# A delta-rule attention fused with a rational MoE: ScalarE's two reads of a unit's h side by side, four buffers for w, u and r, query products two slots later

## The chip, the cores and the metric

One core of a Trainium2 chip runs the whole program. PE is the matrix engine (TensorE), DVE the vector engine (VectorE), ACT the scalar engine (ScalarE), POOL is GpSimd, and SP is the engine that issues nearly all DMAs. Each engine takes its instructions strictly in the order in which they stand in its own queue, and waits for the others through semaphores. The metric is the device time of one execution in microseconds (us).

## The reference

A linear attention with a delta rule runs over 768 tokens for 4 x 8 heads of size 48; its output goes, token by token, through a two-layer network whose activation is a quotient of two polynomials of h.

```python
k_n = k / (norm(k) + 1e-6)
for t in range(S):                                  # S = 768, state is 48 x 48 for each head
    y[t]  = q[t] @ state
    v_old = state @ k_n[t]
    state = state + beta[t] * outer(k_n[t], v[t] - v_old)
x = y as [B * S, H * D]                             # 3072 x 384
h = x @ w_in                                        # 384 -> 2048
P = a0 + a1*h + a2*h**2 + a3*h**3
Q = 1 + |b0|*|h| + |b1|*h**2
out = (P / (Q + 1e-6)) @ w_out                      # 2048 -> 384
```

## The kernel before

The tokens are taken in 12 chunks of 64. A chunk of all heads passes through four pieces of attention code, each cut into 8 slots: `ahead` (loads and normalizes k), `front` (key products, the start of a triangular inverse, scales, transposed queries, query products), `middle` (off-diagonal blocks of the inverse, split of the state, residual, block-diagonal copies made by DMA) and `back` (solve in steps, next state, outputs, tokens, scalars). In one period of 8 slots `back` works on chunk c+1, `middle` on c+2, `front` on c+3 and `ahead` on c+4.

The network is cut into units: unit n is one chunk (256 columns) by 256 of the 2048 hidden features, so there are 8 units for each chunk and 96 in all. A unit is `hidden` (18 matmuls into one PSUM tile `ph`, of which there are two buffers), `numerator`, `quotient`, and `accumulate` (24 matmuls into `po`). The loop at the end writes numerator(n), quotient(n-1), one attention slot, accumulate(n-2) and hidden(n+1), in this order.

In `numerator`, L821 (ACT) reads `ph` and makes z in the buffer `mr`; L823 (DVE) reads z and `ph` and makes w in `mw`; L825 (ACT) reads `ph` and makes u in `mu`; L826 (ACT) takes the absolute value of w; L827 and L828 (DVE) read `ph` again and finish u. In `quotient`, L839 and L840 (ACT) make r by a logarithm and an exponential, in the buffer of z; L843 or L845 (DVE) makes the high half of g in `mg`, L846 (DVE) and L848 (POOL) or L850 (DVE) a remainder, and L851 (POOL) the low half of g. `mw`, `mu` and `mr` have `MB` buffers each; while the weights are loaded, the same three tags take the staged weights.

A scheduler sets the order of each engine's instructions before the program runs: it goes by the data's dependencies, by the buffers that are free, by priorities (code order, moved ahead where `high_priority` stands) and by times that it estimates. It also lets two engines that read the same PSUM tile do so one after the other, in code order. So an edit of a few lines can move instructions anywhere.

Three more tags matter. `g` (one buffer) holds the key products of L516, which two DMAs (L518) copy to DRAM, and later the masked query products `m32` of L655. `u0` (one buffer) holds `et` of L606's six DMAs. `sh` (two buffers) holds the state, split in two halves, which the residual's matmuls `pk` and the output's matmuls `py` read. `pk`, `pu`, `pd` and `py` take turns in one PSUM tile, and `pg`, `pm`, `pe` in another.

Of the kernel before, what the change touches and what calls it, by code (L numbers as in the profile page):

```python
# [10 lines left out]
F16 = mybir.dt.float16  # L11
F32 = mybir.dt.float32
BF16 = mybir.dt.bfloat16
U32 = mybir.dt.uint32
AF = mybir.ActivationFunctionType
# [21 lines left out]
def kernel(  # L37
# [12 lines left out]
    nc = tc.nc  # L50

    B, H, S, D = q.shape
    DM, DFF = moe_w_in.shape
    P = 128
    C = 64
# [7 lines left out]
    HP = NPAIR * H  # L63
# [1 line left out]
    NH = H // HG  # L65
    NG = NPAIR * NH
    TG = NPAIR * P
    MB = 3
    SHIFT = 2
    SHAPE = {  # L70
        "k": [P, NPAIR, 2, NH, 2, C, HG],
# [9 lines left out]
    sb = ctx.enter_context(tc.tile_pool(name="sb", bufs=2))  # L81
# [80 lines left out]
    a0, a1, a2, a3 = (coef[:, i : i + 1] for i in range(4))  # L162
# [60 lines left out]
    def split16(dst, src, scale=None, eng=None):  # L223

        if scale is None:
            nc.scalar.copy(dst[0], src)  # L226
        else:
            nc.scalar.activation(dst[0], src, AF.Copy, scale=scale)
        if scale is None:
            (eng or nc.vector).tensor_sub(dst[1], src, dst[0])  # L230
        else:
            nc.vector.scalar_tensor_tensor(  # L232
                out=dst[1], in0=src, scalar=scale, in1=dst[0], op0=ALU.mult, op1=ALU.subtract
            )
# [62 lines left out]

    STAGES = (("mw", MB), ("mu", MB), ("mr", MB))
    stage = [0]

    def staged(shape, dtype, nm):
        stage[0] += 1
        tag, bufs = STAGES[stage[0] % len(STAGES)]
        return sb.tile(shape, dtype, tag=tag, name=nm, bufs=bufs)
# [4 lines left out]
    def to_f32(t, src, nm, keep=MIN_NORMAL):  # L309

        n = t.shape[-1]
        st = staged([P, n, 2], U32, "ws" + nm)
        nc.sync.dma_start(out=st.rearrange("p f w -> p (f w)"), in_=src)
        wl, wh = st[..., 0], st[..., 1]
        a = sb.tile([P, n], F32, tag="mg", name="wa" + nm, bufs=MB)
        nc.scalar.activation(a, wh.bitcast(F32), AF.Abs)
        nc.gpsimd.tensor_scalar(a, a, 3.0e38, keep, op0=ALU.min, op1=ALU.max)
        nc.vector.tensor_scalar(
            t, a.bitcast(U32), 3, KEEP, op0=ALU.logical_shift_left, op1=ALU.bitwise_and
        )  # L320
        for word, scalar, in1, op0, op1 in (
            (wh, 0xC0000000, t, ALU.bitwise_and, ALU.bitwise_or),
            (wl, 29, t, ALU.logical_shift_right, ALU.bitwise_or),
        ):
            nc.vector.scalar_tensor_tensor(out=t, in0=word, scalar=scalar, in1=in1, op0=op0, op1=op1)  # L325
# [63 lines left out]
    def alternating(t):  # L389

        return t.rearrange("p g x a -> p g a x")

    def mm3(dst, bd, rt, start=True, stop=True):

        for p in PAIRS:
            mm3p(dst, bd, rt, p, start, stop)
# [13 lines left out]
    def bank(pool, nm, w):  # L410

        t = pool.tile([P, NPAIR, 512], F32, tag="a", name=nm)[:, :, : H * w].rearrange("x p (h w) -> x p h w", w=w)
        return t[:, 0], t[:, 1], t
# [5 lines left out]
    def parts_by_pair(t):  # L419
        return by_pair(t[:, 0]), by_pair(t[:, 1])  # L420

    def to_diagonal(nm, t, c=0):
        bd = diag[nm][c % len(diag[nm])]
        for b in range(2):
            sl = slice(b * C, (b + 1) * C)
            if nm == "kn":
                for a in range(HG):
                    nc.sync.dma_start(
                        out=bd[sl].rearrange("t p i (n a) b d -> t (p i n) a b d", a=HG)[:, :, a, b],
                        in_=t[:, :, :, :, a, b].rearrange("p i n t d -> t (p i n) d"),  # L430
                    )
            elif nm in "kq":
                dma = nc.sync.dma_start(
                    out=bd[sl, :, :, :, b].rearrange("x p i n t a -> x (p i n) (t a)"),
                    in_=t[sl].rearrange("x p i n t a -> x (p i n) (t a)"),
                )
                mark(nm + "bd", c, dma)
            elif nm == "w":
                nc.sync.dma_start(out=bd[sl, :, b, : t.shape[2]], in_=t[sl])
            else:  # L440
                nc.sync.dma_start(out=bd[sl, :, :, b, : t.shape[3]], in_=t[sl])
        return bd

    def grouped(t):

        return t.rearrange("p (g a) x -> p g a x", a=HG)
# [146 lines left out]
    def off_blocks(c):  # L593

        d = info[c]
        gbd, wc = d.pop("gbd"), d.pop("wc")
        pe = bank(ps_f, f"pe_{c}", C - 16)
        mm3(pe, gbd, wc[:, :, 16:])
        d["wbd"] = to_diagonal("w", wc)
        et = sb.tile([P, 2, HP, C - 16], F16, tag="u0", name=f"et_{c}", bufs=1)  # L600
        split16(parts_by_pair(et), pe[2], 1.0 / 256.0)
        ebd = d["ebd"] = diag["e"][0]
        for b in range(2):
            for j in range(NB - 1):
                sl = slice(b * C + 16 * j, b * C + 16 * j + 16)
                nc.sync.dma_start(out=ebd[sl, :, :, b, 16 * (j + 1) :], in_=et[sl, :, :, 16 * j :])  # L606
# [42 lines left out]
    def query_products(c):  # L649

        d = info[c]
        pm = bank(ps_f, f"pm_{c}", C)
        mm3(pm, d["kbd"], d["tq"])
        m32 = sb.tile([P, HP, C], F32, tag="g", name=f"m32_{c}", bufs=1)
        nc.vector.tensor_mul(  # L655
            m32, pm[2].rearrange("x p h t -> x (p h) t"), mask.unsqueeze(1).broadcast_to([P, HP, C])
        )
        mm = d["mm"] = sb.tile([P, 2, NG, C, HG], F16, tag="mm", name=f"mm_{c}", bufs=1)
        split16([alternating(mm[:, i]) for i in range(2)], grouped(m32), eng=nc.gpsimd)
# [4 lines left out]
    def state_split(c):  # L664

        d = info[c]
        d["sh"] = sb.tile([P, 2, HP, D], F16, tag="sh", name=f"sh_{c}", bufs=2)
        split16(parts(d["sh"]), S16, d["ss"])

    def residual(c):  # L670
# [142 lines left out]
    def numerator(n):  # L813

        c, f2 = divmod(n, NU)
        d = unit[n]
        A3, B1, A1, B0, A0, Q0 = (toks[c]["m"][:, i, f2 : f2 + 1] for i in range(6))
        ph = d.pop("ph")

        r = z = sb.tile([P, 2, TG], F32, tag="mr", name=f"mr{n}", bufs=MB)  # L820
        nc.scalar.activation(z, ph, AF.Abs, scale=B1)  # L821
        w = sb.tile([P, 2, TG], F32, tag="mw", name=f"mw{n}", bufs=MB)
        nc.vector.scalar_tensor_tensor(out=w, in0=z, scalar=B0, in1=ph, op0=ALU.add, op1=ALU.mult)  # L823
        u = sb.tile([P, 2, TG], F32, tag="mu", name=f"mu{n}", bufs=MB)
        nc.scalar.activation(u, ph, AF.Identity, scale=A3, bias=a2)  # L825
        nc.scalar.activation(w, w, AF.Abs)  # L826
        nc.vector.tensor_mul(u, ph, u)  # L827
        nc.vector.scalar_tensor_tensor(out=u, in0=u, scalar=A1, in1=ph, op0=ALU.add, op1=ALU.mult)  # L828

        by_pool = 2 <= c < NCH - 1 and f2 in (0, 4, 5, 6)  # L830
        if by_pool:
            nc.gpsimd.tensor_scalar(u, u, A0, 1.0, op0=ALU.add, op1=ALU.mult)
        d.update(u=u, w=w, r=r, A0=A0, Q0=Q0, by_pool=by_pool)

    def quotient(n):

        d = unit[n]
        u, w, r, A0, Q0, by_pool = (d.pop(x) for x in ("u", "w", "r", "A0", "Q0", "by_pool"))
        nc.scalar.activation(r, w, AF.Ln, bias=Q0)  # L839
        nc.scalar.activation(r, r, AF.Exp, scale=-1.0)  # L840
        g = sb.tile([P, 2, 2, TG], F16, tag="mg", name=f"mg{n}", bufs=MB)
        if by_pool:
            nc.vector.tensor_mul(g[:, 0], u, r)  # L843
        else:
            nc.vector.scalar_tensor_tensor(out=g[:, 0], in0=u, scalar=A0, in1=r, op0=ALU.add, op1=ALU.mult)  # L845
        nc.vector.scalar_tensor_tensor(out=w, in0=w, scalar=Q0, in1=g[:, 0], op0=ALU.add, op1=ALU.mult)  # L846
        if by_pool:
            nc.gpsimd.tensor_sub(u, u, w)  # L848
        else:
            nc.vector.scalar_tensor_tensor(out=u, in0=u, scalar=A0, in1=w, op0=ALU.add, op1=ALU.subtract)  # L850
        nc.gpsimd.tensor_mul(g[:, 1], u, r)  # L851
        d["g"] = g
# [66 lines left out]
    def front(c, j):  # L919

        if j == 0:
            keys_transposed(c)
        elif j == 1:
            key_products(c)
        elif j == 2:
            invs[c] = inverse(c)
            next(invs[c])
            scales(c)
            queries_transposed(c)
        elif j == 3:  # L930
            next(invs[c])
            query_products(c)
        elif j == 4:
            next(invs[c], None)

    def middle(c, j):

# [66 lines left out]
    for n in range(N + 2):  # L1004
        c, j = divmod(n, NU)
# [38 lines left out]
```

## Time and profile before

| | |
|---|---|
| three runs | 852.14, 852.40, 855.28 us (median 852.4) |
| the profiled execution | 851.81 us, of which 850.1 us are the span from its first to its last instruction |
| granted PE clock, mean | 0.892 of full speed |
| first unit's w (L823) starts | 148.4 us |
| last unit's w (L823) starts | 835.6 us |

A row of the profile names the source line, the engine, the operation, output<-inputs, the number of executions, the busy time, the mean duration in ns, and the idle time of the engine just before, with what ended it. Until about 140 us the kernel loads and splits the weights beside the first chunks' attention; from 140 to about 790 us units and attention run together; after that the last units run alone.

### The profile page before, as it was taken

The numbers are of one execution on the slowest core, as the hardware profiler recorded it, in microseconds if no ns is written. First come the engines' busy times: TensorE is split into PE (matmuls) and PEld (weight loads), VectorE is DVE, ScalarE is ACT, GpSimd is POOL, SyncE is SP. The second block draws the span as 40 slices with busy tenths as digits, with TensorE's granted clock in tenths as the row PEclk, the third lists the DMA queues.
The fourth block names the chain that finished last, engine by engine and source line by source line (L and its number), as shares of the span: only waits on it lengthen the run. The fifth ranks groups of instructions, "written<-read, shape, count | busy, mean of one in ns | idle before, by whom it ended". The sixth has DMA issues, their size and how long they took to land.

```text
span 850.1 us, 23231 instructions
## 1 busy us (share of the span) xinstructions
PE 626.3 (74%) x9264; PEld 492.8 (58%) x9264; DVE 755.3 (89%) x1369; ACT 613.6 (72%) x1278; POOL 423.6 (50%) x394
## 2 busy tenths in 40 slices
PE   0230345777788588787978967978988889999885
PEld 0220344565566376575756845856766767777553
DVE  5999896797989879979999899899799999899896
ACT  4866658777665696686956965976868868887774
POOL 6555754435234425644645464555654556353622
PEclk9855556896899799998989999899999999999999
DMA  8998969679696986988789589479789573300000
GB/s 238 251 202 177 221 154 180 109 167 152 132 133 120 179 144 121 170 145 154 128 143 172 95 162 158 72 138 169 115 170 146 89 146 58 74 2 20 1 19 19
DMA packets 466508, 111.46 MB, mean 131 GB/s; under 512 B 431329, under 2 KB 463073, under 8 KB 466401
## 3 DMA queue, kind: packets, MB, share of 16 engines
q1 hardware_dynamic: 464224, 108.83, 69.8%
q8 instruction: 72, 1.18, 0.6%
q10 hardware_dynamic: 2176, 1.17, 0.5%
q14 instruction: 36, 0.29, 0.1%
HBM read 40.47 MB, written 26.23 MB: 78 GB/s over the span
## 4 chain that ended last, share of the span: by engine, by line
DVE 46%; ACT 16%; DMA 13%; SPq 9%; issue 8%; PE 5%; POOL 2%; POOLq 0%; ACTq 0%; DVEq 0%
DVE mw L846 5%; DVE mw L823 4%; DVE mg L845 4%; DVE w_out L325 4%; DVE mu L827 3%; DVE mu L850 3%; DVE mu L828 3%; SPq L119 3%; DMA xdq<-kn 3%; ACT mu L825 3%; DVE pr L566 2%; PE ph L803 2%; DVE z L232 2%; DMA tk<-xdk 2%; ACT mw L826 2%
## 5 line engine op out<-in xcount | busy, mean ns | idle before, releaser
L866 PE MATMUL po<-w_out,mg 128*128 128x384 f16 x1152 | 222.9, 338 | 26.2 <-POOL mg L851 24.5
L803 PE MATMUL ph<-xT,w_in 128*128 128x256 f16 x1728 | 221.8, 282 | 25.7 <-DVE mu L828 17.6
L803 PEld LDWEIGHTS <-w_in 128*128 128x128 f16 x1728 | 171.6, 101 | 62.9 <-issue 18.7
L851 POOL TENSOR_TENSOR mg<-mu,mr 128x512 f16<-128x512 f32 x96 | 130.6, 1363 | 114.1 <-DVE mu L850 64.5
L866 PEld LDWEIGHTS <-mg 128*128 128x128 f16 x1152 | 110.0, 101 | 97.4 <-POOL mg L851 31.0
L825 ACT ACTIVATE mu<-ph,coef,msc 128x512 f32<-128x512 f32 x96 | 74.6, 777 | 55.2 <-DVE mw L823 54.9
L401 PEld LDWEIGHTS <-kbd 128*128 128x128 f16 x1680 | 61.8, 106 | 45.4 <-issue 33.6
L846 DVE SCALAR_TENSOR_TENSOR mw<-mw,msc,mg 128x512 f32<-128x512 f32 x96 | 87.6, 914 | 0.6
L848 POOL TENSOR_TENSOR mu<-mu,mw 128x512 f32<-128x512 f32 x36 | 48.0, 1334 | 70.6 <-DVE mw L846 48.5
L821 ACT ACTIVATE mr<-ph,msc 128x512 f32<-128x512 f32 x96 | 64.9, 681 | 21.4 <-PE ph L803 9.4
L823 DVE SCALAR_TENSOR_TENSOR mw<-mr,msc,ph 128x512 f32<-128x512 f32 x96 | 70.6, 738 | 10.8 <-ACT mr L821 10.7
L827 DVE TENSOR_TENSOR mu<-ph,mu 128x512 f32<-128x512 f32 x96 | 65.2, 681 | 12.1 <-ACT mu L825 11.9
L828 DVE SCALAR_TENSOR_TENSOR mu<-mu,msc,ph 128x512 f32<-128x512 f32 x96 | 70.7, 738 | 1.1
L839 ACT ACTIVATE mr<-mw,msc 128x512 f32<-128x512 f32 x96 | 69.0, 722 | 0.8
L401 PE MATMUL pu<-z,ebd 128*128 128x48 f16 x1728 | 54.1, 187 | 13.9 <-DVE z L232 9.3
L401 PEld LDWEIGHTS <-ebd 128*128 128x128 f16 x1728 | 53.5, 99 | 17.4 <-issue 15.3
L845 DVE SCALAR_TENSOR_TENSOR mg<-mu,msc,mr 128x512 f16<-128x512 f32 x60 | 57.7, 963 | 5.3 <-ACT mr L840 4.8
L840 ACT ACTIVATE mr<-mr 128x512 f32<-128x512 f32 x96 | 60.0, 629 | 0.6
L826 ACT ACTIVATE mw<-mw 128x512 f32<-128x512 f32 x96 | 59.9, 624 | 0.0
L850 DVE SCALAR_TENSOR_TENSOR mu<-mu,msc,mw 128x512 f32<-128x512 f32 x60 | 54.9, 916 | 0.3
L401 PEld LDWEIGHTS <-wbd 128*128 128x128 f16 x1152 | 35.4, 99 | 33.0 <-issue 31.7
L230 POOL TENSOR_TENSOR mm<-m,mm 128x1024 f16<-128x1024 f32 x12 | 30.3, 2526 | 39.3 <-ACT mm L226 25.7
(198 smaller groups left out, 1287.8 us busy)
## 6 DMA issues: line engine op xcount, KB each, us to landing
wsi<-in_moe_w_in_dram SPq DMA_DIRECT2D x24, 256.0 KB, 5.1
xdk<-kn SPq DMA_DIRECT2D x24, 256.0 KB, 3.7
kbd<-tk SPq DMA_DIRECT2D x24, 256.0 KB, 5.2
gd<-g SPq DMA_DIRECT2D x24, 256.0 KB, 3.6
wso<-in_moe_w_out_dram SPq DMA_DIRECT2D x32, 192.0 KB, 3.9
xdq<-kn SPq DMA_DIRECT2D x24, 256.0 KB, 3.6
mbd<-mm SPq DMA_DIRECT2D x24, 256.0 KB, 6.1
wc<-img SPq DMA_DIRECT2D x24, 256.0 KB, 5.2
```

Source lines behind the costliest of these rows:

```text
L401: nc.tensor.matmul(dst[p][:, h], head(bd, lp, p * H + h), head(rt, rp, p * H + h), start=start and n == 0 and h == 0, stop=stop and n == l ...
L803: nc.tensor.matmul(ph[:, i], w_in[:, f2, wp, cc, i * P : (i + 1) * P], x[:, xp, cc], start=k == 0, stop=k == 3 * NCC - 1,)
L823: nc.vector.scalar_tensor_tensor(out=w, in0=z, scalar=B0, in1=ph, op0=ALU.add, op1=ALU.mult)
L825: nc.scalar.activation(u, ph, AF.Identity, scale=A3, bias=a2)
L826: nc.scalar.activation(w, w, AF.Abs)
L827: nc.vector.tensor_mul(u, ph, u)
L828: nc.vector.scalar_tensor_tensor(out=u, in0=u, scalar=A1, in1=ph, op0=ALU.add, op1=ALU.mult)
L845: nc.vector.scalar_tensor_tensor(out=g[:, 0], in0=u, scalar=A0, in1=r, op0=ALU.add, op1=ALU.mult)
L846: nc.vector.scalar_tensor_tensor(out=w, in0=w, scalar=Q0, in1=g[:, 0], op0=ALU.add, op1=ALU.mult)
L850: nc.vector.scalar_tensor_tensor(out=u, in0=u, scalar=A0, in1=w, op0=ALU.add, op1=ALU.subtract)
L851: nc.gpsimd.tensor_mul(g[:, 1], u, r)
L866: nc.tensor.matmul(po[p], g[:, gp, i, p * P : (p + 1) * P], w_out[:, f2, wp, i], start=f2 == lo and i == 0 and k == 0, stop=f2 == hi - 1 a ...
```

## The change

It has five parts. (1) In `numerator` the line that makes u stands before the line that makes w. In the changed file u is L823 and w is L825; the lines around keep their numbers. (2) `MB` is 4, so `mw`, `mu` and `mr` have four buffers each; `mg` keeps three. (3) `et` moves from the tag `u0` to the tag `g`, so the key products, `et` and `m32` share one buffer. (4) `sh` has one buffer. (5) `query_products` stands in slot 5 of `front` and no longer in slot 3.

```diff
-    MB = 3
+    MB = 4
...
-        et = sb.tile([P, 2, HP, C - 16], F16, tag="u0", name=f"et_{c}", bufs=1)
+        et = sb.tile([P, 2, HP, C - 16], F16, tag="g", name=f"et_{c}", bufs=1)
...
-        d["sh"] = sb.tile([P, 2, HP, D], F16, tag="sh", name=f"sh_{c}", bufs=2)
+        d["sh"] = sb.tile([P, 2, HP, D], F16, tag="sh", name=f"sh_{c}", bufs=1)
...
         nc.scalar.activation(z, ph, AF.Abs, scale=B1)
+        u = sb.tile([P, 2, TG], F32, tag="mu", name=f"mu{n}", bufs=MB)
+        nc.scalar.activation(u, ph, AF.Identity, scale=A3, bias=a2)
         w = sb.tile([P, 2, TG], F32, tag="mw", name=f"mw{n}", bufs=MB)
         nc.vector.scalar_tensor_tensor(out=w, in0=z, scalar=B0, in1=ph, op0=ALU.add, op1=ALU.mult)
-        u = sb.tile([P, 2, TG], F32, tag="mu", name=f"mu{n}", bufs=MB)
-        nc.scalar.activation(u, ph, AF.Identity, scale=A3, bias=a2)
         nc.scalar.activation(w, w, AF.Abs)
...
-        g = sb.tile([P, 2, 2, TG], F16, tag="mg", name=f"mg{n}", bufs=MB)
+        g = sb.tile([P, 2, 2, TG], F16, tag="mg", name=f"mg{n}", bufs=3)
...
         elif j == 3:
             next(invs[c])
-            query_products(c)
         elif j == 4:
             next(invs[c], None)
+        elif j == 5:
+            query_products(c)
```

What the scheduler makes of it is seen at three places. The first is DVE's queue at units 40 and 41, before (`mw40` is unit 40's w, `mu40` its u, `mg40` its g; `pr`, `wt`, `ab` belong to the triangular inverse of chunk 8, `sh_7` is chunk 7's split state):

```order
L823 SCALAR_TENSOR_TENSOR mw40_7847<-mr40_7845,msc_5_7546,ph_40_7826 128x512
L850 SCALAR_TENSOR_TENSOR mu39_7694<-mu39_7694,msc_4_6431,mw39_7692 128x512
L549 TENSOR_TENSOR pr_8_8100<-wt0_111,ab_8_8101 128x16
L232 SCALAR_TENSOR_TENSOR sh_7_8454<-S16_133,sc_7_6807,sh_7_8454 128x768
L550 TENSOR_REDUCE wt0_111<-pr_8_8100 128x4x2
L827 TENSOR_TENSOR mu40_7849<-ph_40_7826,mu40_7849 128x512
L549 TENSOR_TENSOR pr_8_8100<-wt0_111,ab_8_8101 128x36
L823 SCALAR_TENSOR_TENSOR mw41_7975<-mr41_7973,msc_5_7546,ph_41_7954 128x512
L828 SCALAR_TENSOR_TENSOR mu40_7849<-mu40_7849,msc_5_7546,ph_40_7826 128x512
```

And the same place after the change:

```order
L825 SCALAR_TENSOR_TENSOR mw40_7849<-mr40_7845,msc_5_7546,ph_40_7826 128x512
L827 TENSOR_TENSOR mu40_7847<-ph_40_7826,mu40_7847 128x512
L549 TENSOR_TENSOR pr_8_8100<-wt0_111,ab_8_8101 128x36
L825 SCALAR_TENSOR_TENSOR mw41_7977<-mr41_7973,msc_5_7546,ph_41_7954 128x512
L827 TENSOR_TENSOR mu41_7975<-ph_41_7954,mu41_7975 128x512
L828 SCALAR_TENSOR_TENSOR mu40_7847<-mu40_7847,msc_5_7546,ph_40_7826 128x512
L550 TENSOR_REDUCE wt0_111<-pr_8_8100 128x4x3
L828 SCALAR_TENSOR_TENSOR mu41_7975<-mu41_7975,msc_5_7546,ph_41_7954 128x512
L232 SCALAR_TENSOR_TENSOR sh_7_8400<-S16_133,sc_7_6807,sh_7_8400 128x768
```

L827 stands right behind w, where five rows lay between; over all 96 units it stands right behind w in 93, and from w to L828 it is 4.2 rows on average where it was 6.8. The split of chunk 7's state stands behind both units' u.

The second place is ACT's queue at units 42 and 43, before (`y_6` is chunk 6's output, `kn0` the normalized keys):

```order
L821 ACTIVATE mr42_8226<-ph_42_8207,msc_5_7546 128x512
L840 ACTIVATE mr41_7973<-mr41_7973 128x512
L226 CAST kn0_109<-k_9_7654 128x2x8x48
L825 ACTIVATE mu42_8230<-ph_42_8207,coef_99,msc_5_7546 128x512
L826 ACTIVATE mw42_8228<-mw42_8228 128x512
L839 ACTIVATE mr42_8226<-mw42_8228,msc_5_7546 128x512
```

And after:

```order
L821 ACTIVATE mr42_8172<-ph_42_8153,msc_5_7546 128x512
L823 ACTIVATE mu42_8174<-ph_42_8153,coef_99,msc_5_7546 128x512
L840 ACTIVATE mr41_7973<-mr41_7973 128x512
L718 ACTIVATE y_6_8338<-py_6_8241,sc_6_5692 128x768
L821 ACTIVATE mr43_8384<-ph_43_8365,msc_5_7546 128x512
L823 ACTIVATE mu43_8386<-ph_43_8365,coef_99,msc_5_7546 128x512
L826 ACTIVATE mw42_8176<-mw42_8176 128x512
```

u stands right behind z (so in 95 of 96 units), and the instruction that must wait for DVE's w is now L826, with other work between u and it in 86 of 96 units (it stood right behind u in 94).

The third place is DVE's queue where the state of chunk 1 is made (`S16<-pd_1`), before:

```order
L705 SCALAR_TENSOR_TENSOR S16_133<-pd_1_2632,sc_1_1622,S16_133 128x768
L577 TENSOR_SCALAR wh_2_2044<-wt0_111 128x256
L823 SCALAR_TENSOR_TENSOR mw4_2982<-mr4_2980,msc_0_1329,ph_4_2961 128x512
L823 SCALAR_TENSOR_TENSOR mw5_3051<-mr5_3049,msc_0_1329,ph_5_3030 128x512
L578 SCALAR_TENSOR_TENSOR wh_2_2044<-wt0_111,wh_2_2044 128x256
L232 SCALAR_TENSOR_TENSOR sh_2_2841<-S16_133,sc_2_1950,sh_2_2841 128x768
```

And after:

```order
L705 SCALAR_TENSOR_TENSOR S16_133<-pd_1_2578,sc_1_1622,S16_133 128x768
L825 SCALAR_TENSOR_TENSOR mw7_3239<-mr7_3235,msc_0_1329,ph_7_3216 128x512
L827 TENSOR_TENSOR mu7_3237<-ph_7_3216,mu7_3237 128x512
L828 SCALAR_TENSOR_TENSOR mu6_3130<-mu6_3130,msc_0_1329,ph_6_3109 128x512
L492 TENSOR_REDUCE nrm_4_2520<-sq_4_2521 128x16
L828 SCALAR_TENSOR_TENSOR mu7_3237<-mu7_3237,msc_0_1329,ph_7_3216 128x512
```

The state of chunk 1 stood ahead of unit 4 and now stands ahead of unit 7, while unit 8 is the first that needs chunk 1's output. From chunk 5 on the same step stands where it did, within one unit.

The query products have hardly moved in PE's queue: counted in units whose hidden matmuls have begun, `pm` of chunks 1 to 11 began behind 0, 6, 10, 16, 23, 30, 36, 44, 52, 60 and 69 units, and begins behind 0, 6, 10, 18, 23, 28, 36, 44, 52, 60 and 68. Their buffer `mm` was already free only after the DMAs of slot 5.

More of the change, by code (lines that the diff above doesn't have):

```diff
@@ L314, in to_f32 @@
         wl, wh = st[..., 0], st[..., 1]
-        a = sb.tile([P, n], F32, tag="mg", name="wa" + nm, bufs=MB)
+        a = sb.tile([P, n], F32, tag="mg", name="wa" + nm, bufs=3)
         nc.scalar.activation(a, wh.bitcast(F32), AF.Abs)
```

## The prediction

> **What bounds the kernel now.** I read the busy table first, then the span by stage, then what DVE waits for, then the groups of a unit, and last single waits in the timeline. The page's totals and chain:
>
> ```profile
> span 850.1 us, 23231 instructions
> PE 626.3 (74%) x9264; PEld 492.8 (58%) x9264; DVE 755.3 (89%) x1369; ACT 613.6 (72%) x1278; POOL 423.6 (50%) x394
> ...
> DVE 46%; ACT 16%; DMA 13%; SPq 9%; issue 8%; PE 5%; POOL 2%; POOLq 0%; ACTq 0%; DVEq 0%
> ```
>
> The same by stage (columns: window, its length, busy time of PE, PEld, DVE, ACT, POOL, PE clock, DMA share, GB/s):
>
> ```profile
> 0.00:140.00 140.00, 38.03 (x599) 32.18 (x600) 122.17 (x330) 91.61 (x240) 82.19 (x119) 0.66 0.92 206
> 140.00:790.00 650.00, 544.96 (x8357) 431.44 (x8357) 585.78 (x971) 484.20 (x967) 320.02 (x258) 0.93 0.72 126
> 790.00:850.00 60.00, 43.29 (x310) 29.18 (x308) 47.38 (x69) 37.82 (x73) 21.41 (x17) 0.98 0.06 14
> ```
>
> DVE is the bound: it stands still for 850.1 - 755.3 = 94.8 us, of which 17.8 in the first 140, 64.2 in the 650 where the units run beside the attention, and 12.6 in the tail. The change removes no instruction, so it can win only out of these 95 us, or lose by adding to them. What DVE waits for:
>
> ```profile
> DVE mu L827 <- ACT mu L825: 11.9, 15, 2.6
> DVE mw L823 <- ACT mr L821: 10.7, 15, 2.1
> DVE nrm L492 <- ACT sq L491: 7.8, 4, 3.0
> DVE z L232 <- ACT z L228: 5.6, 6, 1.9
> DVE mg L845 <- ACT mr L840: 4.8, 7, 1.5
> ...
> DVE v L676 <- PE pk L401: 3.7, 1, 3.7
> ```
>
> Each row gives the total in us, the number of waits and the longest. The two largest are the two handoffs that part (1) touches. The groups of a unit (busy us, mean ns, idle before, releaser):
>
> ```profile
> L846 DVE SCALAR_TENSOR_TENSOR mw<-mw,msc,mg 128x512 f32<-128x512 f32 x96 | 87.6, 914 | 0.6
> L825 ACT ACTIVATE mu<-ph,coef,msc 128x512 f32<-128x512 f32 x96 | 74.6, 777 | 55.2 <-DVE mw L823 54.9
> L845 DVE SCALAR_TENSOR_TENSOR mg<-mu,msc,mr 128x512 f16<-128x512 f32 x60 | 57.7, 963 | 5.3 <-ACT mr L840 4.8
> L850 DVE SCALAR_TENSOR_TENSOR mu<-mu,msc,mw 128x512 f32<-128x512 f32 x60 | 54.9, 916 | 0.3
> L843 DVE TENSOR_TENSOR mg<-mu,mr 128x512 f16<-128x512 f32 x36 | 29.2, 812 | 4.3 <-ACT mr L840 2.0 <-POOL mu L832 1.5 <-ACT kp L777 0.9
> ```
>
> ACT loses 54.9 us in front of u, though u needs nothing that w makes: it only has to follow DVE's read of the same `ph`. In the timeline one such unit (start, duration, then in brackets the wait):
>
> ```profile
> 465.62 0.73 DVE L823 SCALAR_TENSOR_TENSOR mw<-mr,msc,ph 128x512 f32<-128x512 f32 x1
> 466.38 0.78 ACT L825 ACTIVATE mu<-ph,coef,msc 128x512 f32<-128x512 f32 x1 [4.90 <-DVE mw L823]
> 467.26 0.69 DVE L827 TENSOR_TENSOR mu<-ph,mu 128x512 f32<-128x512 f32 x1 [0.85 <-ACT mu L825]
> ...
> 476.45 0.75 DVE L823 SCALAR_TENSOR_TENSOR mw<-mr,msc,ph 128x512 f32<-128x512 f32 x1 [2.06 <-ACT mr L821]
> ```
>
> ACT stood 4.90 us behind w, DVE then 0.85 us behind u; two units on, DVE stands 2.06 us behind z.
>
> **The change part by part.** *(1) u ahead of w.* DVE's wait in front of L827 goes: u is then done before w may start, and L827 stands right behind w in DVE's queue. That is -11.9 us, and hardly less, since the waits are DVE's own. In its place w waits for u as well as z. u takes 0.78 us (777 ns), so where DVE already waits for z, 15 times, it waits up to 0.78 longer: +11.7 us at most. At least it is 0, because the loop has another side: `ph` is given back when L828 ends, and from w to L828 it is now 4.2 rows where it was 6.8. DVE's mean row is 755.3 / 1369 = 0.55 us, so the buffer comes back about 1.4 us sooner after w, more than the 0.78 that w starts later. PE's waits show that this side counts:
>
> ```profile
> PE ph L803 <- DVE mu L828: 17.6, 18, 4.8
> PE pm L401 <- DMA tq<-xdq: 15.4, 6, 6.4
> PE pk L401 <- ACT y L718: 9.6, 5, 2.4
> ```
>
> I take +3, nearer to zero than to twelve, because 1.4 is more than 0.78. The 54.9 us in which ACT was blocked do not vanish: L826 still waits for w, with the next units' z and u ahead of it. But what stood behind u comes sooner, and DVE's other waits for ACT (7.8 + 5.6 + 4.8 in the rows above, 18.2) should shrink. Between 0 and -12 (two thirds) I take -3, because these rows (squares, solve steps, r) hang on other chains too.
>
> *(2) Four buffers.* Where a buffer of `mr` was missing, z would wait for POOL's L851, which frees it. The trace has that:
>
> ```profile
> L821 ACT ACTIVATE mr<-ph,msc x96: 667/680/707, 147.7 to 834.3; 128x512 f32<-128x512 f32 x96
> ...
>   POOL mg L851: 1.7, 3
> ```
>
> Three waits, 1.7 us, on ACT: worth 0 to -1.7, and I take 0. In the first 140 us the same tags stage the weights, 12 tiles instead of 9, and SP now has the attention's first transfers behind three to five more weight loads. DVE is 122.17 of 140 busy there and its weight instructions are the same: 0, with -3 and +5 as ends, both out of the 17.8 us it idles there.
>
> *(3) and (5) One buffer for the key products, `et` and `m32`.* `et` must wait until both DMAs of the key products have landed, where it needed no more than its own old DMAs:
>
> ```profile
> 480.93 1.03 ACT L516 ACTIVATE g<-pg 128x1024 f32<-128x1024 f32 x1
> 481.99 1.34 SPq L518 DMA_DIRECT2D gd<-g  x2
> 487.25 0.82 ACT L228 ACTIVATE et<-pe 128x768 f16<-128x768 f32 x1
> ...
> 521.12 1.21 DVE L655 TENSOR_TENSOR m<-pm,mask 128x1024 f32<-128x1024 f32 x1
> ...
> gd<-g SPq DMA_DIRECT2D x24, 256.0 KB, 3.6
> ...
> ebd<-et SPq DMA_DIRECT2D x24, 48.0 KB, 2.9
> ```
>
> The second DMA is issued by 483.3 and lands 3.6 us later (median), 486.9; `et` comes at 487.25. So 0.3 us is to spare: cost 0, at worst 1 to 2 us in a few chunks, and on ACT. I take +1. `m32` follows `et` by 34 us here, and the largest of `et`'s DMAs land in 2.9 us, so that is covered. If it were not, DVE would stand in front of L655 with the units' rows behind it. The query products' matmuls stand where they stood (front of this document), so the 15.4 us that PE waits for `tq` stay: 0, at best -4.
>
> *(4) One buffer for `sh`.* Its next half-tiles may be written only when `py` has read the old ones; before, they were written right behind S:
>
> ```profile
> 186.43 1.01 DVE L705 SCALAR_TENSOR_TENSOR S<-pd,sc,S 128x768 f32<-128x768 f32 x1
> 187.48 0.94 ACT L228 ACTIVATE sh<-S,sc 128x768 f16<-128x768 f32 x1
> 187.50 1.55 PE L401 MATMUL py<-sh,qbd 128*128 128x48 f16 x48 [2.94 <-DVE S L705]
> 188.87 2.10 PE L401 MATMUL py<-z,mbd 128*128 128x48 f16 x48
> 190.43 1.01 DVE L232 SCALAR_TENSOR_TENSOR sh<-S,sc,sh 128x768 f16<-128x768 f32 x1
> 192.02 0.90 ACT L718 ACTIVATE y<-py,sc 128x768 f32<-128x768 f32 x1
> ```
>
> The reader `pk` needs not only `sh` but also the PSUM tile that `py` holds until y is evacuated (PE's 9.6 us behind y above). After the 48 matmuls on `sh` that takes 2.10 + 0.90 = 3.0 us; the two writes of `sh` take 0.94 + 1.01 = 1.95. So the new wait hides behind the old one as long as ACT and DVE take these rows within 1.05 us: 0. Without that cover each late microsecond counts once for each of 11 chunks.
>
> *The start.* Chunk 1's state now stands ahead of unit 7, and unit 8 needs its output. From S at 186.43 to y at 192.02 are 5.6 us, and the token scaling comes behind it. DVE has the inverse of chunk 3 and unit 6's and 7's rest to do meanwhile, but not much else. From zero to the 8 us that would be one chain of y, scaling and hidden matmuls with nothing beside it, I take +2, near the one such wait that the trace has (3.7, `v` behind `pk`).
>
> **Sum:** -11.9 + 3 - 3 + 0 + 1 + 0 + 2 = -8.9 us, from 851.8 to 842.9 for an execution like the profiled one. The median of the three runs, 852.4, stands 0.6 above it: **843 us**. The forecast's own range is 836 to 848: the ends of (1) alone span it.
>
> **Rivals.** *The wait only changes its name.* DVE still needs ACT before w, and the planner had placed rows into the gap that is now closed; w's waits grow by all of 11.7: 852.4 - 11.9 + 11.7 + 2 = 854, between 848 and 857. For it: DVE's order is fixed from estimates, and what one wait releases the next one takes. Against it: three handoffs for a unit (w, L827, L843 or L845) become two.
>
> *More than the sum.* ACT no longer blocked takes two thirds of the 18.2, `ph` back sooner takes half of w's 10.7: 852.4 - 11.9 - 12 - 5 + 3 = about 826. Against it: 64.2 us idle are all there is in the middle, and half of them would have to go.
>
> *DVE slowed by POOL.* DVE's rows with both tensors in SBUF are often stretched, those that read `ph` never:
>
> ```profile
> L846 DVE SCALAR_TENSOR_TENSOR mw<-mw,msc,mg x96: 657/746/2736, 159.5 to 841.1; 128x512 f32<-128x512 f32 x96
> L823 DVE SCALAR_TENSOR_TENSOR mw<-mr,msc,ph x96: 721/738/749, 148.4 to 835.6; 128x512 f32<-128x512 f32 x96
> ```
>
> Minimum, median and maximum in ns: mean less median, times the count, is 16.1 us for L846 (914 - 746, 96 times); with medians like it L845 gives 13, L850 10 and L843 (median near 0.68) 5: 44 us in DVE's 755. If `ph` reads now stand together, the other four stand together too, beside POOL's L848 and L851. Should the stretch grow by a third, 15 us, the result is 843 + 15 = 858, slower than before; it outweighs the gain from a fifth (9 of 44) on. Against it: the number and length of POOL's reads is unchanged. The Trainium skill, page "SBUF — State Buffer", section "Who interferes with whom", says that a VectorE instruction with two SBUF inputs and a GpSimd instruction that reads SBUF block each other, and one with at most one does not; the trace agrees (maximum 2736 against 749 ns). By that rule time depends on which of the two starts first, which the change shifts in either direction.
>
> *The state's chain.* If `sh` is taken late by 2.5 us, 1.5 beyond its cover, in 11 chunks, that is +16, or 859. For it: the split now stands behind two units' u in DVE's queue. Against it: `pk` follows in PE's queue at the same unit from chunk 5 on.
>
> **How the numbers follow.** Forecast 0.50; more than the sum 0.11; changed name 0.20; POOL's stretch 0.11; the state's chain 0.08. About 0.5%, 4.3 us, is what a measurement of this kernel can tell from no change, so "same" is 848.1 to 856.7. Faster is the first two, 0.61; the changed name is the same, 0.20; the last two give 0.19. The range leaves out a tenth at either end: most of "more than the sum" below 828, and the upper half of the last two above 860.
>
> **What would show it.** Right: no row of DVE's L827 waiting for ACT; w (L825) behind u at 10 to 17 us; ACT's 54.9 moved to L826 and smaller; DVE idle near 86 us with busy time within 5 us of 755. PE's wait for `ph` below 17.6. Wrong: DVE's busy time up by 10 or more (stretch); `pk` waiting for `sh`, or ACT's `et` for the key products' DMA; a hole in DVE around 200 us; or w's wait above 22.6 us, the sum of the two old ones.

## The result, and the profile after

The changed kernel takes 863.9 us (median of 4 runs, 859.2 to 870.4) against 852.3 before on the same chip: a ratio of 1.013, 95% interval 1.010 to 1.017. In a second comparison, with ten runs, it was 859.7 against 852.1: 1.010 (1.007 to 1.013). The forecast was 843 us.

The profiled execution of the first comparison ran at a granted clock of 0.79 where all other executions of this kernel had 0.87 to 0.94, so the profile read below is that of the same kernel in the second comparison: 865.4 us at a clock of 0.915, 5.8 above its median. Its totals and chain:

```profile
span 863.5 us, 23249 instructions
PE 634.2 (73%) x9264; PEld 500.9 (58%) x9264; DVE 755.3 (87%) x1369; ACT 617.4 (72%) x1278; POOL 431.3 (50%) x394
...
DVE 35%; PE 17%; ACT 15%; DMA 11%; issue 10%; SPq 6%; POOL 5%; ACTq 0%; POOLq 0%; DVEq 0%
```

DVE works as long as before (755.3 us); all that was lost is idle time, 108.2 us instead of 94.8. The execution at 0.79 had 751.2 us busy and 117.5 idle, so two executions of one kernel can differ by 4 us in DVE's busy time and by 9 in its idle time. By stage (columns as before):

```profile
0.00:140.00 140.00, 39.09 (x599) 33.08 (x600) 126.09 (x331) 92.61 (x242) 82.04 (x120) 0.90 0.88 200
140.00:790.00 650.00, 537.18 (x8274) 428.67 (x8274) 570.92 (x953) 477.89 (x948) 322.61 (x255) 0.92 0.73 127
790.00:870.00 80.00, 57.95 (x394) 39.14 (x391) 58.25 (x87) 46.94 (x89) 26.70 (x21) 0.92 0.04 10
```

In the first 140 us DVE idles 3.9 less (13.9 instead of 17.8), in the 650 where units and attention share it 14.9 more (79.1 instead of 64.2), in the tail 2.5 more (15.2 instead of 12.7). The waits, each with total, number and longest:

```profile
POOL mg L851 <- DVE mu L850: 108.2, 33, 12.0
...
ACT mw L826 <- DVE mw L825: 59.4, 40, 3.7
...
DVE mw L825 <- ACT mu L823: 22.5, 20, 1.8
...
PE ph L803 <- DVE mu L828: 19.1, 9, 3.6
...
DVE mg L845 <- ACT mr L840: 14.9, 12, 4.2
```

The same waits in the execution at 0.79:

```profile
ACT mw L826 <- DVE mw L825: 46.7, 36, 3.5
...
DVE mw L825 <- ACT mu L823: 27.3, 26, 2.0
...
PE ph L803 <- DVE mu L828: 16.1, 8, 3.0
DVE mg L845 <- ACT mr L840: 14.9, 9, 5.7
```

And the groups of a unit, again at 0.915:

```profile
L825 DVE SCALAR_TENSOR_TENSOR mw<-mr,msc,ph 128x512 f32<-128x512 f32 x96 | 70.9, 739 | 22.9 <-ACT mu L823 22.5
L846 DVE SCALAR_TENSOR_TENSOR mw<-mw,msc,mg 128x512 f32<-128x512 f32 x96 | 86.5, 904 | 0.4
L845 DVE SCALAR_TENSOR_TENSOR mg<-mu,msc,mr 128x512 f16<-128x512 f32 x60 | 58.4, 975 | 15.1 <-ACT mr L840 14.9
L827 DVE TENSOR_TENSOR mu<-ph,mu 128x512 f32<-128x512 f32 x96 | 65.3, 680 | 0.0
L850 DVE SCALAR_TENSOR_TENSOR mu<-mu,msc,mw 128x512 f32<-128x512 f32 x60 | 57.6, 961 | 0.3
```

L827 waits for nothing, as the change says. But w now waits 22.5 us in the one execution and 27.3 in the other, and the two old waits, 10.7 for z and 11.9 for u, were 22.6 together. So nothing was won: the wait has moved to w. ACT is still blocked by w, now in front of L826, for 59.4 or 46.7 us instead of 54.9. DVE's wait for r at L845 went from 4.8 to 14.9 in both.

### The profile page after: what moved, and what is told of

It reads as the page before. It is cut to its first block, busy times and chain, and to the rows that moved or that the text cites. A ratio compares the mean times of both kernels' runs of the same rounds, so it can differ in the third digit from the quotient of the medians.

```text
span 868.7 us, 23249 instructions
## 1 busy us (share of the span) xinstructions
PE 673.8 (78%) x9264; PEld 516.4 (59%) x9264; DVE 751.2 (86%) x1369; ACT 620.4 (71%) x1278; POOL 432.3 (50%) x394
## 4 chain that ended last, share of the span: by engine, by line
PE 34%; DVE 26%; DMA 10%; ACT 9%; issue 8%; SPq 8%; POOL 4%; ACTq 0%; POOLq 0%; DVEq 0%
PE ph L803 12%; PE po L866 12%; PE pu L401 3%; DVE w_out L325 3%; DVE mg L845 2%; DVE mw L846 2%; POOL mg L851 2%; DMA kbd<-tk 2%; DVE mu L850 2%; SPq L119 1%; PE pg L401 1%; DMA gb<-gd 1%; DVE mu L827 1%; SPq L606 1%; DMA xdq<-kn 1%
## 5 line engine op out<-in xcount | busy, mean ns | idle before, releaser
L803 PE MATMUL ph<-xT,w_in 128*128 128x256 f16 x1728 | 247.5, 303 | 21.1 <-DVE mu L828 16.1
L866 PE MATMUL po<-w_out,mg 128*128 128x384 f16 x1152 | 246.8, 365 | 19.1 <-POOL mg L851 17.4
L803 PEld LDWEIGHTS <-w_in 128*128 128x128 f16 x1728 | 182.9, 107 | 71.5 <-issue 13.4
L851 POOL TENSOR_TENSOR mg<-mu,mr 128x512 f16<-128x512 f32 x96 | 134.4, 1402 | 127.6 <-DVE mu L850 100.4
L866 PEld LDWEIGHTS <-mg 128*128 128x128 f16 x1152 | 116.6, 106 | 102.4 <-POOL mg L851 21.7
L825 DVE SCALAR_TENSOR_TENSOR mw<-mr,msc,ph 128x512 f32<-128x512 f32 x96 | 71.0, 740 | 27.7 <-ACT mu L823 27.3
L826 ACT ACTIVATE mw<-mw 128x512 f32<-128x512 f32 x96 | 60.3, 631 | 47.1 <-DVE mw L825 46.7
L846 DVE SCALAR_TENSOR_TENSOR mw<-mw,msc,mg 128x512 f32<-128x512 f32 x96 | 86.0, 899 | 0.4
L401 PEld LDWEIGHTS <-kbd 128*128 128x128 f16 x1680 | 64.5, 106 | 27.6 <-issue 24.9
L823 ACT ACTIVATE mu<-ph,coef,msc 128x512 f32<-128x512 f32 x96 | 74.3, 774 | 0.0
L845 DVE SCALAR_TENSOR_TENSOR mg<-mu,msc,mr 128x512 f16<-128x512 f32 x60 | 56.8, 948 | 16.2 <-ACT mr L840 14.9
L828 DVE SCALAR_TENSOR_TENSOR mu<-mu,msc,ph 128x512 f32<-128x512 f32 x96 | 70.6, 737 | 0.2
L848 POOL TENSOR_TENSOR mu<-mu,mw 128x512 f32<-128x512 f32 x36 | 50.8, 1411 | 33.4 <-DVE mw L846 16.5
L827 DVE TENSOR_TENSOR mu<-ph,mu 128x512 f32<-128x512 f32 x96 | 65.4, 682 | 0.0
L401 PE MATMUL pu<-z,ebd 128*128 128x48 f16 x1728 | 56.0, 187 | 5.4 <-DVE z L232 5.4
L401 PEld LDWEIGHTS <-wbd 128*128 128x128 f16 x1152 | 37.3, 100 | 36.1 <-issue 34.7
L832 POOL TENSOR_SCALAR mu<-mu,msc 128x512 f32<-128x512 f32 x36 | 30.8, 855 | 50.8 <-DVE mu L828 43.2
```

What stands on the lines that cost most here:

```text
L401: nc.tensor.matmul(dst[p][:, h], head(bd, lp, p * H + h), head(rt, rp, p * H + h), start=start and n == 0 and h == 0, stop=stop and n == l ...
L803: nc.tensor.matmul(ph[:, i], w_in[:, f2, wp, cc, i * P : (i + 1) * P], x[:, xp, cc], start=k == 0, stop=k == 3 * NCC - 1,)
L866: nc.tensor.matmul(po[p], g[:, gp, i, p * P : (p + 1) * P], w_out[:, f2, wp, i], start=f2 == lo and i == 0 and k == 0, stop=f2 == hi - 1 a ...
```

## Experiments

In the table, "idle" is the span less DVE's busy time, both from the page's first lines. Ratios are to the kernel before, on the same chip; medians of two rows can come from different chips, on which the kernel before differs by up to 1 us. The last column is of one profiled execution, up to 6 us from the median.

| kernel | median us | ratio (95%) | span, DVE busy, idle |
|---|---|---|---|
| before | 851.3 to 852.3 | 1 | 850.1, 755.3, 94.8 |
| whole change, again | 859.7 | 1.010 (1.007 to 1.013) | 863.5, 755.3, 108.2 |
| part 1 alone | 855.4 | 1.005 (1.002 to 1.008) | 859.3, 750.3, 109.0 |
| parts 2 to 5 | 847.6 | 0.994 (0.992 to 0.997) | 846.2, 756.0, 90.2 |
| part 5 alone | 850.9 | 0.999 (0.996 to 1.003) | 850.5, 756.9, 93.6 |
| whole change, u first from unit 16 on | 861.2 | 1.011 (1.008 to 1.014) | 859.4, 754.3, 105.1 |
| whole change, u first in units 0 to 15 | 855.7 | 1.005 (1.003 to 1.007) | 853.0, 752.2, 100.8 |
| parts 1, 3, 4, 5 | 861.7 | 1.011 (1.007 to 1.015) | 860.0, 761.6, 98.4 |
| parts 2 to 5, u last | 846.5 | 0.994 (0.992 to 0.996) | 847.7, 746.1, 101.6 |
| whole change, w from z alone | 868.8 | 1.019 (1.017 to 1.022) | 866.0, 790.4, 75.6 |
| whole change, short u | 849.9 | 0.997 (0.995 to 0.999) | 845.5, 748.1, 97.4 |
| parts 2 to 5, short u | 849.8 | 0.998 (0.997 to 1.000) | 847.1, 759.2, 87.9 |
| parts 3, 4, 5 | 836.3 | 0.982 (0.979 to 0.984) | 837.5, 751.7, 85.8 |
| parts 1, 3, 4, 5, short u | 855.0 | 1.003 (1.001 to 1.005) | 852.0, 747.0, 105.0 |
| parts 3, 4, 5, short u | 843.6 | 0.989 (0.986 to 0.992) | 841.9, 751.0, 90.9 |
| parts 3, 4 | 835.2 | 0.981 (0.977 to 0.984) | 839.6, 744.4, 95.2 |
| parts 3, 4, 5, u last | 862.4 | 1.011 (1.009 to 1.014) | 863.1, 760.4, 102.7 |
| part 3 alone | 844.0 | 0.992 (0.989 to 0.995) | 842.2, 753.8, 88.4 |
| part 4 alone | 850.3 | 0.998 (0.995 to 1.000) | 847.3, 748.5, 98.8 |

**Which part loses.** The whole change once more, part 1 alone (u's two lines moved ahead of w's), all but part 1, and part 5 alone (query products from slot 3 to slot 5).

> The changed kernel once more, to have a profile at the granted clock of the one before (0.89), since its first profile has 0.79. Theory A, part (1) or the others make DVE wait longer whatever the clock: the time stays at 860 to 865 us, DVE idles 105 us or more (94.8 before), and w waits for u about as in the first profile (27 us). Theory B, the loss is the lower clock: at a clock near 0.89 the time falls to 852 or below and DVE idles less than 95 us.

> Part (1) alone, u ahead of w; three buffers, all else as before. If the wait for u in front of w is what costs (theory A1), it is slower by most of the loss, 858 to 864 us. If the loss comes from the shared buffers and the later query products (theory A2), part (1) alone gives the forecast's gain of it, -11.9 + 3 - 3: about 841 us, 836 to 848.

> Parts (2) to (5) without (1): four buffers, one shared buffer g, one sh, query products in slot 5; w still ahead of u. Theory A1: about as before, 849 to 856 us, and the two waits for z and u stay at 20 to 24 us in sum. Theory A2: as slow as the whole change or slower, 862 to 875 us.

> Part (5) alone, the query products' code two slots later; their buffer was free only then, so by the prediction they hardly move: 852 us, within 4. Theory A2 with the query products as its cause: 858 us or more.

At a clock of 0.915 the whole change is still 1.0% slower, so the clock isn't the reason (theory B falls). Part 1 loses by itself (+3.3 us) and beside the others (859.7 - 847.6 = +12.1); the others gain 4.5 without it. That is the direction of theory A1, though both kernels are 1 to 3 us below what it gave them, and part 1 alone shows less than half of the loss where it was to show most of it. The waits for z and u in parts 2 to 5 were to stay at 20 to 24 us and are 18.1, since u's is only 4.3 there:

```profile
DVE mw L823 <- ACT mr L821: 13.8, 20, 1.5
...
DVE mg L845 <- ACT mr L840: 5.0, 7, 1.5
DVE mu L827 <- ACT mu L825: 4.3, 10, 0.8
```

Part 5 does nothing that can be measured.

**A hole, or every unit?** Busy time by stretch, of the kernel before, of parts 2 to 5, and of the whole change (columns: window, length, busy time and number of instructions of PE, PEld, DVE, ACT, POOL, then clock and DMA):

```profile
140.00:240.00 100.00, 76.91 (x1183) 62.65 (x1183) 85.66 (x158) 71.98 (x159) 39.97 (x32) 0.83 0.81 141
```

```profile
140.00:240.00 100.00, 77.68 (x1218) 63.51 (x1218) 86.06 (x154) 73.88 (x159) 40.15 (x32) 0.86 0.91 147
...
340.00:440.00 100.00, 82.92 (x1360) 66.59 (x1360) 86.44 (x141) 72.96 (x147) 50.95 (x41) 0.88 0.88 151
```

```profile
140.00:240.00 100.00, 70.26 (x1102) 58.12 (x1102) 76.97 (x151) 69.67 (x151) 36.00 (x31) 0.82 0.85 147
```

DVE is busy 8.7 us less than before in these 100 us (76.97 against 85.66), more than half of the 14.9 that the middle lost. There, with u first, the steps of chunk 3's inverse stand on DVE in one piece ahead of unit 8. Its w in the timeline of parts 2 to 5 (two rows in one, units 8 and 9), and of the whole change:

```profile
221.42 1.41 DVE L823 SCALAR_TENSOR_TENSOR mw<-mr,msc,ph 128x512 f32<-128x512 f32 x2 [0.81 <-ACT mr L821]
```

```profile
232.59 0.74 DVE L825 SCALAR_TENSOR_TENSOR mw<-mr,msc,ph 128x512 f32<-128x512 f32 x1
```

It starts 11 us later. Two mirror images of the whole change tell a local hole from a cost of each unit:

```diff
+        u_first = n >= 16      # the mirror: n < 16
+        if u_first:
             u = ...; nc.scalar.activation(u, ph, AF.Identity, scale=A3, bias=a2)
         w = ...
+        if not u_first:
+            u = ...; nc.scalar.activation(u, ph, AF.Identity, scale=A3, bias=a2)
```

> All five parts, but u ahead of w only from unit 16 on; units 0 to 15 keep w ahead of u. Its plan is that of parts 2 to 5 alone up to unit 16. Theory H (the loss is one hole: at the first boundary of chunks the order of VectorE, written anew because of part 1, puts unit 7's last steps and all of unit 8 behind the inverse of chunk 3 and the state of chunk 2, and VectorE idles about 11 us between 205 and 232 us): 848 to 853 us, and unit 8's w starts at about 221 us. Theory D (every unit's w pays for its wait for u, 12 us over 96 units): 855 to 859 us, since 80 of 96 units still pay.

> The mirror image: u ahead of w in units 0 to 15 only, all else as in the whole change. Theory H: 856 to 861 us, nearly the whole loss, with unit 8's w at about 232 us. Theory D: 848 to 851 us, since only 16 of 96 units pay.

> Parts 1, 3, 4 and 5 with three buffers for w, u and r. Part 1 holds in every unit, but on VectorE the order at the first boundary is again state, unit 6, unit 7, and unit 8 and 9 stand among the inverse's steps instead of behind them. Theory H: 847 to 853 us, no hole. Theory D: 854 to 860 us.

> Parts 2 to 5, and u moved the other way: ScalarE's order is z, abs of w, u, so that w waits for nothing but z, the logarithm's input comes first and VectorE's product with u waits longer. At the boundary, unit 8 and 9 follow unit 7 without the inverse between. Theory H: 846 to 853 us, wherever u stands. Theory D, in which what counts is how soon w is done: 840 to 847 us, better than 847.6 with w between the two reads.

Theory H, the hole, fell. With u first from unit 16 on, DVE fills the first stretch again and loses in another; the columns are as above, the kernel is that one:

```profile
140.00:240.00 100.00, 76.19 (x1167) 62.08 (x1167) 84.51 (x149) 73.75 (x159) 39.98 (x32) 0.86 0.92 146
...
340.00:440.00 100.00, 83.25 (x1415) 67.81 (x1414) 80.62 (x132) 72.16 (x148) 50.09 (x41) 0.91 0.89 155
```

Parts 2 to 5 had 86.44 in that second stretch, as the row above shows. The time is 861.2, the whole loss without the hole, above both theories' ranges. The mirror keeps the hole (unit 8's w at 232.2 us) and is at 855.7, above theory D's 848 to 851 and 0.3 below theory H's range, so it alone would have spoken for H. Together they show neither a hole nor an equal share for each unit: the two losses over parts 2 to 5, 13.6 and 8.1, add up to more than the 12.1 of the whole. Parts 1, 3, 4 and 5 start unit 8's w at 223.9 us and lose too (861.7). And parts 3, 4 and 5, one of the two fastest kernels below, have DVE busy only 74.5 us between 140 and 240, less than the whole change with its 77.0: a hole there need not cost time in the end. u last (846.5) lies in both theories' ranges and is level with w between the reads. There ACT begins w's absolute value 0.56 us behind w's end instead of 1.30 (means over the 96 units of the two traces), but r is done no sooner, 5.0 us behind w instead of 4.9.

**Taking the wait away.** In the first kernel w no longer reads h: `in1=z` in place of `in1=ph`. In the next two u's read is one column. These three leave a part of the network's function out and serve as experiments only. The fourth is parts 3, 4 and 5 as they are.

```diff
-        nc.scalar.activation(u, ph, AF.Identity, scale=A3, bias=a2)
+        nc.scalar.activation(uc, ph[:, 0, :1], AF.Identity, scale=A3, bias=a2)
...
-        nc.vector.tensor_mul(u, ph, u)
+        nc.vector.tensor_mul(u, ph, uc.unsqueeze(2).broadcast_to([P, 2, TG]))
```

> All five parts, but w is made from z alone, (z + B0) times z instead of times h (so the sums that follow have other values): VectorE's w no longer reads h, so nothing sets w and u in an order, and the code's two orders give one and the same program. Theory D (the loss is w's wait for the read of u, 0.7 us of ScalarE ahead of each w): 840 to 848 us, at or below the 847.6 of parts 2 to 5, with VectorE's waits for z and u together under 18 us. Theory O (ScalarE's two reads side by side are themselves the worse order of work, whoever waits): 852 to 862 us if the program keeps them side by side.

> All five parts, but u's read takes one column of h instead of 512 (the product on VectorE then uses that column for all; this frees some 50 us of ScalarE too). w still waits for u. Theory D: the wait costs next to nothing when the read is short, so this is within 3 us of its mirror r3_ut_old, both 836 to 847. Theory O: 8 us or more above r3_ut_old.

> Parts 2 to 5 with w ahead of u, and the same short read of u. Theories D and O: 836 to 847, at or a little below the 847.6 with the full read; it is the mirror for r3_ut_new.

> Parts 3, 4 and 5 with three buffers for w, u and r, w ahead of u. If the fourth buffer is what parts 2 to 5 gain by (4.5 us): 850 to 855 us. If it is the earlier start (state and query products placed otherwise while the weights are staged): 845 to 849 us, with VectorE again busy about 77 us between 60 and 140 us.

The first came out at 868.8, above both theories' ranges. Its groups of w and its waits:

```profile
L825 DVE SCALAR_TENSOR_TENSOR mw<-mr,msc 128x512 f32<-128x512 f32 x96 | 102.8, 1071 | 7.5 <-ACT mr L821 7.3
```

```profile
DVE mg L845 <- ACT mr L840: 7.6, 9, 2.0
DVE mw L825 <- ACT mr L821: 7.3, 11, 1.4
```

With no wait between w and u, DVE's waits for the pair fall from 22.5 to 7.3, under the 18 of theory D, those of L845 from 14.9 to 7.6, and the idle time from 108.2 to 75.6. The edit itself made w longer, 102.8 us instead of 70.9, and DVE 790.4 busy. So DVE idles 32.6 us less but works 35.1 more. Longer rows hide waits, so the run does not show what the dependence costs, neither in its idle time nor in its total: the experiment brought a cost of its own.

The short reads with four buffers are level, 849.9 and 849.8, as theory D had it, but both are 3 us above its 836 to 847. The short read also takes 34 and 39 us off ACT's busy time, so a shorter wait isn't all that it changes; with w first the kernel is no faster for it (847.6 with the full read). And the idle times of the two aren't level, 97.4 and 87.9; the one with u first merely had 11 us less busy time. And parts 3, 4 and 5 at 836.3 were outside everything that had been expected: beside them, part 1 costs 25.4 us, and the fourth buffer 847.6 - 836.3 = 11.3.

**With three buffers.**

> Parts 1, 3, 4 and 5 with three buffers, and u's read cut to one column of h. With the full read part 1 costs 25 us here (861.7 against 836.3). Theory D (the length of the read that w waits for): within 4 us of r4_ut3_old. Theory O (the order itself, and what the planner makes of it): 10 us or more above it.

> Parts 3, 4 and 5 with three buffers, w ahead of u, and the same short read of u. Theories D and O: 832 to 845 us, near the 836.3 with the full read. If it is above 848 us, the 836.3 was one lucky order of the work, and no size below some 12 us can be put down to one edit.

> Parts 3 and 4 alone: the shared buffer for et and one buffer for sh, with query products in their old slot. If the sharing brings the 15 us of parts 3 to 5: 834 to 842 us. If only the sharing with the later query products does: 848 to 856 us (part 5 alone was 850.9).

> Parts 3, 4 and 5 with three buffers, and ScalarE's order z, abs of w, u. With four buffers this order was level with w between the reads (846.5 against 847.6). If the place of u behind w doesn't matter: 833 to 842 us. If the product's wait for u counts (11.4 us of it with four buffers): 843 to 850 us.

The short read with u first is 11.4 us above its mirror: theory O's 10 us or more, not theory D's 4, though less than half of the 25 with the full read. The mirror itself, 843.6, lies in its range. Part 1 has now been put beside five settings:

| setting | time without, with u first | difference | idle without, with | difference |
|---|---|---|---|---|
| alone | 852.1, 855.4 | +3.3 | 94.8, 109.0 | +14.2 |
| parts 2 to 5 | 847.6, 859.7 | +12.1 | 90.2, 108.2 | +18.0 |
| parts 3 to 5 | 836.3, 861.7 | +25.4 | 85.8, 98.4 | +12.6 |
| parts 2 to 5, short u | 849.8, 849.9 | +0.1 | 87.9, 97.4 | +9.5 |
| parts 3 to 5, short u | 843.6, 855.0 | +11.4 | 90.9, 105.0 | +14.1 |

DVE's idle time rises by 9 to 18 us in all five, with the full read and with the short one. Each idle time is of one execution, and two executions of the whole change were 9 us apart, so the sizes are rough; that all five have the same sign is the finding. The times scatter between 0 and 25 because DVE's busy time moves as well, by -11 to +10 us, with the same 1,369 instructions, and because the profiled executions are not the median ones. So theory D holds only for a part: by the times, the length of the read is worth 12.1 - 0.1 = 12.0 and 25.4 - 11.4 = 14.0 us, but by the idle times 8.5 and -1.5, which the idle times are too rough to tell from nothing. What holds in every pair is that u ahead of w leaves DVE idle for longer, however short the read.

Of the parts that gain, 3 and 4 alone give 835.2: the later query products add nothing. u last with three buffers is 26 us slower than w between the reads, far above both of its ranges, where with four buffers it was level. Why is not known.

**Which shared buffer.**

> Part 3 alone: et in the buffer of the key products. The prediction put it at +1 us. If sharing et's buffer brings the 16 us that parts 3 and 4 bring together (835.2): 834 to 841 us. If one buffer for sh does: 849 to 856 us. If the 16 us belongs to neither edit but to the order that the pair happens to give: both alone between 842 and 858.

> Part 4 alone: one buffer for sh instead of two, put at 0 us in the prediction. The same three cases: 849 to 856 us, 834 to 841 us, or between 842 and 858 for both.

Part 3 alone gains 8.1 us, part 4 alone 1.8 (not told from none), both together 16.2. That is the third case: both alone lie between 842 and 858. So some half of the gain goes with `et` in the key products' buffer, and the rest only comes about when both are there. How a buffer that is *shared* makes the kernel faster is not settled. A part of it shows in the first 140 us, where DVE is busy 124.9 us with part 3 and was 122.2 before. Nor is the gain of one kind: in the profiles part 3 alone has 6.4 us less idle time and 1.5 less busy time than the kernel before, parts 3 and 4 have 0.4 more idle and 10.9 less busy.

## Why the prediction was wrong, step by step

**(1) L827's wait goes, -11.9.** Right against the kernel before: 0.0 is left. But beside parts 2 to 5 there were only 4.3 us of it to win.

**(1) w also waits for u, +3 between 0 and +11.7.** This step failed: 22.5 less 10.7 is +11.8, a little above its upper end, and in the other execution it was +16.6. The end was 15 old waits times 0.78 us; but DVE waited 20 and 26 times, and up to 2.0 us at once. Two parts of the working came true: w starts 0.8 us later behind z (2.55 us after z's start instead of 1.77, means over the 96 units of the traces), and `ph` is given back 1.8 us sooner after w (4.46 us to the end of L828 before, 2.69 now), even more than the 1.4 reckoned. What did not follow is a gain on PE's side: its wait for `ph` is 19.1 us in the one execution and 16.1 in the other, where it was 17.6. The first rival, "the wait only changes its name", had this term at 11.7 and was given 0.20; its 848 to 857 us was still too low.

**(1) DVE's other waits for ACT, -3 between 0 and -12.** Failed in its sign: the three rows named (7.8, 5.6 and 4.8) are now 3.6, 6.4 and 14.9, together 24.9 instead of 18.2 (26.6 in the other execution). Those of them that are not shown above, from DVE's waits in the whole change:

```profile
DVE z L232 <- ACT z L228: 6.4, 7, 2.3
...
DVE nrm L492 <- ACT sq L491: 3.6, 2, 2.6
```

The premise was right: what ACT makes behind u does come sooner. r is done 4.2 us after w's end instead of 5.1. What the prediction left out is that DVE comes to it sooner still, because its own order has less between. From w to L845 or L843 of the same unit DVE had 11.3 rows on average and now has 9.8, and the next unit's w stood ahead of that row in 62 of 95 units, now in 50. The units overlap less. All five pairs above have this in common (11.1 to 11.7 rows and 54 to 68 units without, 9.6 to 9.9 and 42 to 51 with u first). Their waits, and the mean time from w's end to r and to DVE's use of it, each without and with u first:

| setting | DVE's waits for z and u, us | its waits for r, us | r is done after, us | DVE uses it after, us |
|---|---|---|---|---|
| alone | 22.6, 18.9 | 6.8, 12.8 | 5.1, 4.4 | 6.8, 5.7 |
| parts 2 to 5 | 18.1, 22.5 | 5.9, 18.0 | 4.9, 4.2 | 7.0, 5.9 |
| parts 3 to 5 | 14.3, 21.1 | 6.0, 8.1 | 5.3, 4.1 | 7.1, 5.6 |
| parts 2 to 5, short u | 12.5, 14.5 | 4.9, 7.7 | 4.2, 3.5 | 6.5, 5.5 |
| parts 3 to 5, short u | 15.6, 10.4 | 6.4, 9.7 | 4.3, 3.8 | 6.4, 5.6 |

The waits for z and u together rise in three pairs and fall in two; those for r rise in all five, and the time between r and its use shrinks by 0.3 us in all five. These rows do not make up the whole rise of the idle time: with part 1 alone they give 2.3 of 14.2 us, and DVE's waits for PE rise there from 6.1 to 16.8. So it is seen that less work between w and r's use goes with the idle time; that it is the cause stays open, since one order of the queues with the other order of the reads was not tried.

**(2) Four buffers, 0.** Wrong with w between the reads: parts 3 to 5 are 836.3 with three and 847.6 with four, +11.3. With u first it is -2.0 (861.7 and 859.7).

**(3) et's buffer, +1.** Wrong: -8.1 alone. That ACT's `et` doesn't wait for the key products' transfers was right; a row for it doesn't appear. `m32` behind `et`'s transfers cost 4.1 us once, in parts 2 to 5. **(4) One sh, 0**: -1.8 alone, not told from 0. `pk` waits 5.3 us for `sh` in the whole change, three times, and 4.5 less for y than it did (5.1 instead of 9.6): the cover that was named holds there but for 0.8 us in all, and in parts 2 to 5 but for 2.7 (3.1 for `sh`, 9.2 for y). **(5) Query products, 0**: right, -1.2 alone, within 0.5%.

**The start, +2.** The first 140 us, which stood under (2) with -3 as the better end, idle 3.9 us less. The hole near 200 us that was a sign of being wrong did come: DVE is busy 8.7 us less than before between 140 and 240, more than the 8 us that the term had as its end. But kernels without it lost as much, so what it costs in the end is not known.

**The sum of 2 to 5 with the start** was put at +3 and measured -4.5; part 1 was put at -11.9 and measured +12.1 beside them. The whole miss of 16.7 us (859.7 against 843) is part 1's 24.0 less the 7.5 that the others gave, to 0.2.

**The rivals.** "More than the sum" had nothing to it. "DVE slowed by POOL" did not decide this change: busy time is 755.3 before and 755.3 or 751.2 after. The four rows it named did grow, from 229.4 us in all to 238.0 (232.7 in the other execution), but other rows shrank by as much. Among the other kernels busy time scatters from 744.4 us for parts 3 and 4 to 761.6 for parts 1, 3, 4 and 5, and it does so in rows with both tensors in SBUF: L846 takes 80.7 us in the one and 93.7 in the other, L828, which reads `ph`, 71.0 and 70.4. "The state's chain" is refuted by parts 2 to 5, which have the single `sh` and gain. Of the signs of being wrong that were named ahead, three appeared: `pk` waiting for `sh`, the hole, and, in one of two executions, w's wait above 22.6 us.

Two kernels found on the way beat both by most: parts 3 and 4, 0.981 (0.977 to 0.984), and parts 3, 4 and 5, 0.982 (0.979 to 0.984). The page of the second:

```profile
span 837.5 us, 23243 instructions
...
PE 625.8 (75%) x9264; PEld 494.8 (59%) x9264; DVE 751.7 (90%) x1369; ACT 613.7 (73%) x1278; POOL 424.4 (51%) x394
```

## What to carry to other kernels

Where two engines read one buffer by turns, swapping the turns need not remove the wait: in three of five settings here DVE's waits for the two reads grew, in two they shrank, and in none did they go. A forecast should also ask what stands between a value's start and its use in the queue of the engine that sets the pace: here the value was ready sooner, and its user waited longer. Where a planner orders the queues, every edit rewrites them (with the one buffer count of part 4 some 450 of DVE's 1,369 rows in the trace stand in another order), so an edit's effect is only known beside several other sets of edits; here part 1 cost 0 to 25 us in time, and only the sign of its effect on the idle time of the bounding engine was steady. A change of several parts is measured by leaving each out: one of the two best kernels of this study was two of the five parts.

## What was not expected of the hardware

w with both tensors in SBUF took 1,071 ns on average (727 to 2,847, median 745), and with `ph` in PSUM as one of them 739 (749 at most, in the prediction's row): the row of the longer w above is the test of the prediction's stretch on a row that differs in that one input. The traces show who the other party is. In the kernel with the longer w all 34 w's over 800 ns begin while a POOL instruction runs, and each ends 537 to 552 ns after the end of one; of the 62 shorter ones 6 begin so. In the kernel before, all 21 rows of L846 over 800 ns begin while a POOL instruction runs, and end 542 to 551 ns after the end of one; of the 75 shorter ones 8 begin so. The Trainium skill, page "SBUF — State Buffer", section "Who interferes with whom", says that a VectorE instruction with two SBUF inputs contends with a GpSimd instruction that reads SBUF and one with at most one doesn't; this pair agrees.

The changed kernel ran at 870.4 us with a granted clock of 0.79 in the first comparison and at 865.4 with 0.915 in the second (spans 868.7 and 863.5). PE's busy time differs by 39.6 us between these two, the span by 5.2. The first one's page has:

```profile
span 868.7 us, 23249 instructions
...
PE 673.8 (78%) x9264; PEld 516.4 (59%) x9264; DVE 751.2 (86%) x1369; ACT 620.4 (71%) x1278; POOL 432.3 (50%) x394
```
